# Splitting the first sequence of a fused SSD and MLP kernel into two-token and four-token row groups, with a new instruction order

## The chip, the cores and the metric

The kernel runs on one core of one Trainium2 chip. The metric is the device time of one execution in microseconds. The program has five instruction streams: TensorE (PE, with its weight loads shown as PEld), VectorE (DVE), ScalarE (ACT), GpSimd (POOL) and SyncE (SP), of which SP issues nearly all DMAs.

## The reference

A scan over a sequence with decay (a state-space model in chunked form) feeds a two-layer MLP. There are 4 sequences (`batch`) of 768 tokens and 8 heads; a head has 32 channels of x and 16 states for B and C.

```python
log_a = np.log(np.clip(a, 1e-06, 1.0))
for c in range(nc):                       # chunks of 32 tokens
    cum = np.cumsum(la, axis=-1)
    L = np.exp(cum[:, :, :, None] - cum[:, :, None, :]) * causal
    M = np.einsum('bhin,bhjn->bhij', Cc, Bc) * L
    y_intra = np.einsum('bhij,bhjd->bhid', M, xc)
    y_inter = np.einsum('bhin,bhnd->bhid', Cc, state) * np.exp(cum)[:, :, :, None]
    y[:, :, sl] = y_intra + y_inter
    state = decay_full[:, :, None, None] * state + np.sum(Bx, axis=2)
...
x = y.transpose(0, 2, 1, 3).reshape(3072, 256)
h = x @ w_in                              # 256 x 2048
g = 0.5 * h * (1.0 + np.tanh(c * (h + 0.044715 * h * h * h)))
out = g @ w_out                           # 2048 x 256
```

All inputs and the output are float32 in DRAM.

## The kernel before, in words

The kernel takes chunks of 128 tokens, 24 in all, 6 for each sequence, and works on units `u` of two chunks (12 units, three for each sequence).

**Decay.** Instead of logarithms, the kernel multiplies the clipped `a` from the end of a chunk backwards with one scan (`f_Rq`, `f_R`, line 339). The product R scales B, its reciprocal scales C. `turn` (line 350) transposes 32x32 blocks so that tokens come to lie on partitions. The product over a whole chunk reaches all partitions by a small matmul (`f_ppq`, `f_pp`) and is copied to `pendq` or `pend`; it carries the state from chunk to chunk.

**B and C of the first sequence** are handled in two groups, `GR = ((0, 4), (4, 2))`. Group 0 is chunks 0 to 3 in rows of four tokens: partition p holds tokens 4p to 4p+3, so that a DMA row is 256 bytes. `load_bc0` (149) loads, `f_mulc` and `f_mulb` (417, 424) scale, `f_tw` (429) transposes on TensorE, and `f_ew` (437) copies the result out of PSUM and puts the tokens back in order. Group 1 is chunks 4 and 5 in rows of two tokens (`load_bc1`, `f_mul1`, `f_T1`, `f_ce1`, `f_bh1`, `f_N1`, `f_bn1`, lines 153 and 442 to 475). x of chunks 0 to 3 comes in one load of 512-byte rows in the four-token layout (`load_x4`, 182); a cast makes it bf16 (`f_x4`), `f_XX` (563) puts it in token order by matmuls with a selection matrix `unp`, `f_XD` (575) makes the state products directly from the four-token rows, and `f_xn` copies x out of PSUM.

**The second sequence** scales on POOL or DVE (`f_mul`, 479), transposes on TensorE (`f_T`), copies out (`f_E`), splits C into even and odd heads (`f_F`, 519), transposes B back (`f_N`) and copies (`f_bn`). The third and fourth (`XB`) write the scaled B and C to DRAM (`load_wr`), and read them back transposed (`load_tr`) and plain (`load_bn`).

**One unit** is then: `G` (599), the products of B and C in banks ga and gb; `M` (612), the causal mask on DVE, or for unit 0's second half a copy on ACT (`GE`) and a mask on POOL (`ME`); `D` (629), the state products; `S` and `SP` (677, 689), the running state and its block-diagonal copy; `Y` (642), the output of the scan; `yev` (673), the copy to `xm`. For units 4 to 11, D and G of the next unit are issued together with Y.

**The MLP** of one unit is 8 groups `s1` (708), each of 4 matmuls into one of two PSUM buffers `hp`, each followed by a gelu on ACT (720), and 8 groups `s2` (725), each of 4 matmuls that add into an output bank `o_ps` or `yb`; `oev` copies the output, `store` writes it. The weights come in four quarters each of w_in and w_out (`load_wi`, `load_wo`) and are cast to bf16 in halves (`f_wi`, `f_wo`).

**The order** is written out by hand: `ORDERED` (line 17) names the steps in the order in which they are issued. Each engine takes its own steps in that order. A suffix `:A`, `:D` or `:P` puts a step on ACT, DVE or POOL instead of its usual engine; `~n` is a fill of TensorE with n blocks of 128 columns of zeros, and `+n` puts such a fill ahead of an `s1`. SP's DMAs are issued in the list's order too. There are 192 groups s1 and s2.

Of the kernel before, what the change touches and what calls it, by code (L numbers as in the profile page):

```python
# [8 lines left out]
FP32 = mybir.dt.float32  # L9
# [14 lines left out]
load_bc1.0 load_wo.0 wi.3.0:D gelu.0.1 wi.2.1 s1.0.3 load_x.2 SP.2 pe wi.3.1 gelu.0.2 load_bc.1.1  # L24
gelu.0.3 tp6.2 s1.0.4 load_bc.1.0 gelu.0.4 load_x.3 load_wo.1 xn.3 s1.0.5 s1.0.6 Y.1 gelu.0.5 pp
tp2 gelu.0.6 tp6.3 recip1 s1.0.7 S.1.1 yev.1.0.2 mul1.0:P mul1.1:P tp6.1 pend gelu.0.7 s1.1.0
wo.0.1 T1.0 s1.1.1 T1.1 gelu.1.0 bh1 N1 gelu.1.1 s1.1.2 tp6.0 s1.1.3+10 bn1 ce1.1 load_wo.2
castx.2.None SP.3 wo.0.0 ce1.0 gelu.1.2 gelu.1.3 G.2 s1.1.4 recip.1.4 s1.1.5 gelu.1.4 M.2.1
mul.1.1:P s2.0.0.0.o D.2 M.2.0 load_x.4 gelu.1.5 s2.0.1.0.o s1.1.6 T.1.1 gelu.1.6 S.2.0 s1.1.7
SP.4 Y.2 mul.1.0 yev.2.0.2:D gelu.1.7 wo.1.0 wo.1.1 T.1.0 E.1.1:A castx.3.None:A s1.2.0 wo.2.0  # L30
s1.2.1 E.1.0 wo.2.1 load_wo.3 load_bc.2.1 N.1 gelu.2.0 F.1 s1.2.2 bn.1:D G.3 gelu.2.1 gelu.2.2 D.3
s1.2.3 s2.0.0.1.o S.3.0 S.3.1 load_bc.2.0 gelu.2.3 s1.2.4 M.3.1 s2.0.1.1.o s1.2.5 SP.6 gelu.2.4
s1.2.6 M.3.0 gelu.2.5 wo.3.0:D gelu.2.6 s2.0.0.2.o castx.4.None s1.2.7 Y.3 gelu.2.7 wo.3.1:D
s2.0.1.2.o S.4.0 yev.3.0.2 S.4.1 s2.0.0.3.o oev.0 load_x.5 s1.3.0 s1.3.1 mul.2.1 s2.0.1.3.o
load_wr.2.1 load_x.6 gelu.3.0 gelu.3.1 s1.3.2 oev.1:D SP.8 s1.3.3 s2.1.0.0.o gelu.3.2 M.4.0
gelu.3.3 SP.7 s2.1.0.1.o s2.1.0.2.o s2.1.0.3.o oev.2:D s1.3.4 s1.3.5 s2.1.1.0.o gelu.3.4 M.4.1
mul.2.0:P castx.5.None:A s2.1.1.1.o Y.4 S.5.0 s2.1.1.2.o load_wr.2.0 s2.1.1.3.o load_tr.2.1
load_bn.2 oev.3:D gelu.3.5 s1.3.6 s1.3.7 s2.2.0.0.o yev.4.0.2 load_tr.2.0 gelu.3.6 s1.4.0 SP.9
M.5.1 gelu.3.7 s2.2.0.1.o store.0 store.2 gelu.4.0 s1.4.1 castx.6.None:A s1.4.2 SP.10 s2.2.0.2.o
load_x.7 s2.2.0.3.o gelu.4.1 oev.4:D gelu.4.2 s1.4.3 s1.4.4 load_bc.3.1 s2.2.1.0.o s2.2.1.1.o  # L40
s2.2.1.2.o gelu.4.3 gelu.4.4 s2.2.1.3.o s1.4.5 oev.5 s1.4.6 gelu.4.5 M.5.0 s2.3.0.0.o F.2 store.1
Y.5 s2.3.0.1.o s2.3.0.2.o yev.5.0.2 gelu.4.6 s2.3.0.3.o s1.4.7 S.6.0 gelu.4.7 load_bc.3.0 S.6.1
store.3 s1.5.0 oev.6:D SP.12 s2.3.1.0.o gelu.5.0 s1.5.1 s2.3.1.1.o gelu.5.1 castx.7.None:A
mul.3.1:P s2.3.1.2.o s1.5.2 gelu.5.2 M.6.1 s2.3.1.3.o s1.5.3 M.6.0 Y.6 oev.7:D S.7.0 gelu.5.3
load_x.8 s1.5.4 S.7.1 s2.4.0.0.o s2.4.0.1.o s1.5.5 SP.13 gelu.5.4 load_wr.3.1 yev.6.0.2
castx.8.None store.4 load_x.9 gelu.5.5 SP.14 s2.4.0.2.o s2.4.0.3.o oev.8 s1.5.6 s1.5.7 mul.3.0
castx.9.None s2.4.1.0.o gelu.5.6 load_wr.3.0 gelu.5.7 M.7.0 s2.4.1.1.o s1.6.0 M.7.1 load_tr.3.1
# [38 lines left out]
def kernel(  # L86
# [14 lines left out]
    Q = 128  # L101
# [12 lines left out]
    GR = ((0, 4), (4, 2))  # L114
    R4 = GR[0][1]
    XB = (2, 3)
    P4 = Q // R4

# [88 lines left out]
    bmask = const.tile([128, H * D], BF16, name="bmask")
# [776 lines left out]
```

## Time and profile before

| | us |
|---|---|
| three timed runs | 118.32, 118.58, 119.0 |
| their median | 118.58 |
| span of the profiled execution (first to last instruction) | 116.9 |
| TensorE busy | 110.1 (94%) |
| VectorE busy | 69.4 (59%) |
| ScalarE busy | 72.1 (62%) |
| GpSimd busy | 21.4 (18%) |
| first s1 matmul | 12.50 |
| last s2 matmul's end | 113.9 |

The profile gives the span of the one profiled execution and no other time for it; the median of the timed runs is 1.68 us longer than that span. All times inside the profile count from the span's start. Lines L12 are lines of the kernel before; a busy TensorE includes the fills. In rows of the timeline the first number is the start, the second the length; what stands in brackets is the idle time before the row and what ended it.

### The profile page before, as it was taken

The page shows a single profiled execution, that of the slowest core. Times are in us where ns is not written, and L with a number is a line of the kernel's source. Part 1 is how long each engine was busy: PE and PEld are TensorE (multiplying, and loading weights), DVE is VectorE, ACT ScalarE, POOL GpSimd, SP SyncE. Part 2 cuts the span into 40 slices and gives each one's busy share as a digit, 9 for nine tenths or more (in the row PEclk, how much of TensorE's full clock was granted, in tenths as well). Part 3 has the DMA queues.
Part 4 walks back from the last instruction along what each step waited for, and adds up shares of the span by engine and source line. Part 5 has one row for each costly group of instructions (what it writes and reads, how often), then busy time and mean ns, then how long its engine had stood idle before and what let it go on. Part 6 is the DMA issues. An engine that isn't in the chain of part 4 may idle for free.

```text
span 116.9 us, 3379 instructions
## 1 busy us (share of the span) xinstructions
PE 110.1 (94%) x1426; PEld 92.0 (79%) x1426; DVE 69.4 (59%) x140; ACT 72.1 (62%) x139; POOL 21.4 (18%) x38
## 2 busy tenths in 40 slices
PE   6988999998899999999999999999999999999990
PEld 2354676776789979989898999889798998999970
DVE  5898899899785936716695583049493462101020
ACT  2249899968486459565766677828465587447501
POOL 7606816908206000052200000000000000000000
PEclk9999999999999999999999999999999999999999
DMA  0999997999983929998407472044201201101113
GB/s 26 228 332 357 281 252 178 208 288 257 305 143 90 185 47 219 213 253 200 72 25 171 121 163 63 0 140 98 40 6 63 71 0 52 43 0 50 45 47 132
DMA packets 43007, 15.97 MB, mean 137 GB/s; under 512 B 36657, under 2 KB 41457, under 8 KB 42993
## 3 DMA queue, kind: packets, MB, share of 16 engines
q1 hardware_dynamic: 42800, 15.64, 56.0%
q8 instruction: 11, 0.18, 0.6%
q10 hardware_dynamic: 192, 0.13, 0.5%
q14 instruction: 4, 0.02, 0.1%
HBM read 11.04 MB, written 3.93 MB: 128 GB/s over the span
## 4 chain that ended last, share of the span: by engine, by line
PE 75%; DMA 8%; DVE 6%; SPq 6%; issue 2%; POOL 1%; ACT 0%; DVEq 0%; POOLq 0%
PE o_ps L735 33%; PE hp L717 30%; DMA bcf<-in_B_dram 8%; PE yb L735 3%; SPq L190 3%; PE ga L603 3%; PE yb L658 2%; DVE m L613 2%; PE yb L667 2%; DVE ce L523 1%; SPq L150 1%; DVE bh L327 1%; DVE bc L484 1%; SPq L159 1%; SPq L183 1%
## 5 line engine op out<-in xcount | busy, mean ns | idle before, releaser
L721 ACT ACTIVATE gT<-hp 128x512 bf16<-128x512 f32 x96 | 54.3, 596 | 25.0 <-PE hp L717 24.6
L717 PE MATMUL hp<-xm,w_in_sb 128*128 128x256 bf16 x384 | 53.3, 273 | 0.6 <-ACT gT L721 0.4
L735 PE MATMUL o_ps<-w_out_sb,gT 128*128 128x256 bf16 x352 | 47.3, 273 | 0.0
L717 PEld LDWEIGHTS <-w_in_sb 128*128 128x128 bf16 x384 | 41.4, 114 | 3.5 <-issue 1.9
L735 PEld LDWEIGHTS <-gT 128*128 128x128 bf16 x384 | 37.0, 98 | 4.9 <-issue 1.1
L327 DVE COPY o_sb<-o_ps 128x256 f32<-128x256 f32 x13 | 5.5, 425 | 23.8 <-PE o_ps L735 20.4
L613 DVE TENSOR_TENSOR m<-ga,tri 128x1024 bf16<-128x1024 f32 x12 | 14.6, 1218 | 0.1
L613 DVE TENSOR_TENSOR m<-gb,tri 128x1024 bf16<-128x1024 f32 x11 | 13.4, 1219 | 0.7 <-PE gb L603 0.7
L323 ACT ACTIVATE o_sb<-o_ps 128x256 f32<-128x256 f32 x9 | 3.5, 385 | 9.2 <-PE o_ps L735 9.2
L705 PE MATMUL yb<-wz 128*128 128x512 bf16 (+3 forms) x23 | 7.6, 481 | 1.1 <-DVE wz L220 1.1
L691 DVE SCALAR_TENSOR_TENSOR sp_new<-s_new,pend,bmask 128x256 bf16<-128x256 f32 x17 | 7.9, 476 | 0.0
L327 DVE CAST xm<-yb 128x512 bf16<-128x512 f32 x6 | 4.1, 687 | 5.8 <-PE hp L636 4.8
L684 DVE SCALAR_TENSOR_TENSOR s_new<-s_new,pend,hp 128x64 f32<-128x64 f32 x13 | 3.6, 279 | 6.4 <-PE hp L636 6.2
L705 PEld LDWEIGHTS <-wz 128*128 128x128 bf16 x26 | 3.0, 120 | 5.1 <-issue 3.2
L667 PE MATMUL yb<-m,x 128*32 128x128 bf16 x192 | 6.1, 220 | 0.0
L603 PE MATMUL ga<-ce,bh 32*128 32x256 bf16 x48 | 4.7, 273 | 1.3 <-DVE bn L327 0.9
L484 POOL TENSOR_TENSOR bc<-bc_t,pt 128x768 bf16<-128x768 f32 x2 | 3.0, 1494 | 13.8 <-DMA bc_t<-in_C_dram 13.7
L658 PE MATMUL yb<-ce,sp_new 128*32 128x128 bf16 x160 | 5.3, 221 | 0.0
L603 PE MATMUL gb<-ce,bh 32*128 32x256 bf16 x48 | 4.7, 273 | 0.0
L735 PE MATMUL yb<-w_out_sb,gT 128*128 128x256 bf16 x32 | 4.6, 273 | 0.0
L667 PEld LDWEIGHTS <-x 128*32 128x32 bf16 x192 | 3.8, 97 | 0.8 <-issue 0.8
L323 ACT ACTIVATE xm<-yb 128x512 bf16<-128x512 f32 x6 | 3.6, 595 | 1.1 <-PE hp L636 1.1
(115 smaller groups left out, 79.5 us busy)
## 6 DMA issues: line engine op xcount, KB each, us to landing
out_dram<-o_sb SPq DMA_DIRECT2D x24, 128.0 KB, 1.9
x_t<-in_x_dram SPq DMA_DIRECT2D x20, 128.0 KB, 3.9
wf<-in_moe_w_in_dram SPq DMA_DIRECT2D x4, 512.0 KB, 6.7
wf<-in_moe_w_out_dram SPq DMA_DIRECT2D x4, 512.0 KB, 5.5
bc_t<-in_C_dram SPq DMA_DIRECT2D x3, 384.0 KB, 5.8
bc_t<-in_B_dram SPq DMA_DIRECT2D x3, 384.0 KB, 5.5
scr<-bc SPq DMA_DIRECT2D x4, 192.0 KB, 2.2
x_t<-in_x_dram SPq DMA_DIRECT2D x1, 512.0 KB, 5.8
```

Of the source, the lines that this page charges most:

```text
L323: nc.scalar.activation(o, i, AF.Copy)
L327: nc.vector.tensor_copy(out=o, in_=i)
L484: (nc.gpsimd if eng == "POOL" else nc.vector).tensor_tensor(out=d["bc16"][:, i], in0=d["bc"].rearrange("p i h (r n) -> p i r h n", r=R6)[: ...
L603: nc.tensor.matmul(out=gbank(g)[:, 256 * k:256 * k + 256], lhsT=bh_of(2 * u + k)[gs], rhs=ce_of(2 * u + k)[gs], start=True, stop=True, til ...
L613: nc.vector.tensor_tensor(out=m_of(u)[:, 2 * i:2 * i + 2].rearrange("p g k e t -> p (g k e) t"), in0=gx[i].rearrange("p g (k t) -> p (g k) ...
L658: nc.tensor.matmul(out=y4[32 * j:32 * j + 32, k, w], lhsT=sp[:, 32 * h:32 * h + 32], rhs=ce_of(gc)[:, h % 2], start=first(j), stop=False, ...
L667: nc.tensor.matmul(out=y4[32 * j:32 * j + 32, k, w], lhsT=X16[u][:, k, 32 * h:32 * h + 32], rhs=m[:, h // 2, h % 2, :], start=first(j), st ...
L691: nc.vector.scalar_tensor_tensor(out=sp_new.rearrange("p (g d) -> p g d", g=4), in0=(XN[0][:, H * D:H * D + 64] if gc == 0 else state[("s" ...
L705: nc.tensor.matmul(out=t[:, 0:m * 128], lhsT=wz, rhs=w3.to_broadcast([128, m, 128]), start=True, stop=True, skip_group_check=True)
L717: nc.tensor.matmul(out=hp[:, j * T:(j + 1) * T], lhsT=w_in_k[:, w, q, k], rhs=xm[:, w, u * T:(u + 1) * T], start=(w == 0), stop=(w == 1))
L721: nc.scalar.activation(gts[u][:, 2 * i:2 * i + 2], hps.pop((u, i)).rearrange("p (j t) -> p j t", j=2), AF.Gelu_apprx_tanh)
L735: nc.tensor.matmul(out=ops[gc], lhsT=gts[u][:, fi, k * Q:(k + 1) * Q], rhs=w_out_sb[:, fi, :], start=(fi == 0 and (u > 0 or k == 0)), stop ...
```

## The change

The two groups of the first sequence become `GR = ((0, 2), (2, 4))`: chunks 0 and 1 in rows of two tokens (128 bytes), chunks 2 to 5 in rows of four (256 bytes). x is loaded in token order for every chunk, one load of 128-byte rows for each chunk, so `load_x4`, `f_x4`, `unp`, `c_unp`, `f_XX`, `f_XD` and `f_xn` go; units 0 and 1 use `f_castx` and `f_D` like all others, and chunks 0 and 1 get a transposed-back B (`f_N0`, `f_bn0`). The decays of both groups come from one load each of `aq`, with two clips and two scans; the first sequence no longer needs the long scan. For the other sequences `a` is loaded in four overlapping quarters of 192 to 256 tokens on SP, later than before; one scan over 128 partitions and one `turn` serve all (before: 64 partitions, four turns for `rt` and four for the first sequence). The steps of group 1 are halves (`f_mul1`, `f_ce1`, `f_bh1`, `f_N1`, `f_bn1`). Unit 1 also masks its second half by GE and ME; Y and yev of unit 0 are two halves each. `SP` may run on POOL as two instructions. s2 of unit 1 takes its quarters in turns for its two chunks, as unit 0's did, into bank yb. `ORDERED` is another list.

```diff
-load_aq.0 load_aq.1 load_aq.2 load_aq.3 c_wz load_bc0.1 c_ident c_m4 c_sel c_tri c_zero load_bc0.0
-c_unp load_a.0:A clipq load_x4 Rq tpq recip0 c_cz mulc.0 ~59 tw.1 load_wi.0 c_warm load_a.1:A
-ew.1.1:A mulc.1 c_bmask c_m8 tw.2 mulb ~4 tw.0 peq ew.0.2:A clip ew.0.1 load_wi.1 ew.0.0:A ew.1.2
-c_par ~2 G.0 x4.1 ew.1.0 M.0.0 ~1 ppq GE.2 pendq x4.0:P XX.0 ME.2 XD.0 GE.3 xn.1 ME.3 xn.0:D
-load_wi.2 SP.0 ~17 Y.0 wi.0.1:A wi.0.0:A S.0.0 yev.0.0.2 wi.1.1 XX.1 wi.1.0:A R XD.1 S.0.1
-load_wi.3 S.1.0 s1.0.0 SP.1 xn.2 load_bc1.1 wi.2.0 gelu.0.0 G.1 s1.0.1 s1.0.2 M.1.1 M.1.0
...
+c_wz load_aq.0 c_ident load_aq.1 c_zero c_az c_sel load_aq.3 load_aq.2 c_bmask clipq.0 c_warm
+clipq.1 Rq.0 c_m16 tpq.0 c_cz Rq.1 recipq.0 c_selp load_bc0.1 load_bc0.0 c_m4 peq.0 mulc.1
+load_x.0.0 load_bc1.1 c_tri mulc.0:P ~40 load_x.0.1 mulb tpq.1 tw.2 castx.0.0:D peq.1 recipq.1 ew.2
+tw.0 load_bc1.0 tw.1 ew.1:A ppq.0 ew.0:A ~10 N0 G.0 load_wi.0 load_wi.1 bn0:D mul1.1.0:P mul1.1.1:P
+M.0.0 pendq.0 GE.0.3 castx.0.1:D ~19 T1.1 ~2 D.0 GE.0.2 load_x.1.0 ME.0.3 mul1.0.1 mul1.0.0:P c_par
+SP.0 ~13 T1.0 ce1.0.1:D ce1.0.0:D ME.0.2 load_x.1.1 bh1.1 load_wi.2 S.0.0 Yw.0.0 Yw.0.1 ppq.1 bh1.0
+S.0.1 wi.0.1:D G.1 pendq.1:D yev.0.1.2 yev.0.0.1 M.1.0 wi.0.0 s1.0.0+7 GE.1.2 s1.0.1 load_wi.3
+GE.1.3 ~3 N1.0 wi.1.0:D ce1.1.0:D bn1.0:D gelu.0.0 gelu.0.1 load_wo.0 castx.1.0:A wi.1.1 s1.0.2
+gelu.0.2 load_x.2.0 N1.1 SP.1:P castx.1.1 ~4 D.1 ce1.1.1 S.1.0 s1.0.3+2 gelu.0.3 bn1.1:D G.2 SP.2
+S.1.1 wi.2.1:D load_x.2.1 ME.1.3 ME.1.2 M.2.1 wi.3.1:D wi.2.0 wi.3.0 wo.0.0:D M.2.0 Y.1 s1.0.4+2
+s1.0.5 yev.1.0.2 load_wo.1 wo.0.1 gelu.0.4 gelu.0.5 s1.0.6+7 gelu.0.6 s1.0.7 s2.0.0.0.o load_a.3
+load_a.1 load_wo.2 s1.1.0 s2.0.1.0.o castx.2.None:D gelu.0.7 D.2 gelu.1.0 s1.1.1 load_a.2 load_a.0
+gelu.1.1 S.2.0 SP.4 s1.1.2 load_bc.1.0 wo.1.1:D SP.3:P Y.2 yev.2.0.2:D wo.1.0 s1.1.3 c_ends
+load_bc.1.1 s2.0.0.1.o load_wo.3 gelu.1.2 s1.1.4 gelu.1.3 s2.0.1.1.o wo.2.0:D gelu.1.4 s2.1.0.0.o
+wo.2.1:A s2.1.1.0.o s1.1.5 s2.0.0.2.o clip load_x.3.0 s2.1.0.1.o s1.1.6 s2.0.1.2.o gelu.1.5 R
+load_x.4.0 pe load_x.3.1 s1.1.7 tp6 s2.1.1.1.o gelu.1.6 s2.1.0.2.o mul.1.0 load_x.4.1 gelu.1.7
+wo.3.0 T.1.0 s1.2.0 recip.1 gelu.2.0 s1.2.1 mul.1.1 gelu.2.1 T.1.1 E.1.0 s2.1.1.2.o pp N.1 E.1.1
+wo.3.1:A load_bc.2.1 bn.1:D F.1 s1.2.2 pend castx.3.None:D s2.1.0.3.o s1.2.3 gelu.2.2 s2.0.0.3.o
+s2.0.1.3.o gelu.2.3 oev.2:D castx.4.None G.3 D.3 S.3.0 S.3.1 oev.0 oev.1 s1.2.4 s2.1.1.3.o gelu.2.4
...
-    GR = ((0, 4), (4, 2))
-    R4 = GR[0][1]
+    GR = ((0, 2), (2, 4))
+    R2, R4 = GR[0][1], GR[1][1]
...
     def load_bc0(i):
-        nc.sync.dma_start(out=BC0[0][:, i], in_=(B, C)[i][0, :, 0:R4 * Q, :]
-                          .rearrange("h (p r) n -> p h (r n)", r=R4))
+        nc.sync.dma_start(out=BC0[0][:, i], in_=(B, C)[i][0, :, 0:R2 * Q, :]
+                          .rearrange("h (p r) n -> p h (r n)", r=R2))
...
-    def load_x4():
-        nc.sync.dma_start(out=x4_t, in_=x[0, :, 0:R4 * Q, :].rearrange("h (p r) d -> p h (r d)", r=R4))
...
+        nc.sync.dma_start(out=XF[u][:, k], in_=x[b, :, (c + k) * Q:(c + k + 1) * Q, :]
+                          .rearrange("h p d -> p h d"))
...
+    def c_selp(eng):
+        copy(eng, selp, sel8.rearrange("p (h o) -> p h o", o=1).to_broadcast([128, H, N]))
...
+    def f_N0():
+        t = pso.tile([128, 512], FP32, name="o_ps")
+        T0[("n", 0)] = t.bitcast(BF16)[:, 0:R2 * 128]
+        for c in range(R2):
+            nc.tensor.transpose(out=T0[("n", 0)][:, c * 128:(c + 1) * 128],
+                                in_=bh0[0][:, c * Q:(c + 1) * Q], identity=ident)
...
-    def f_mul1(i, eng):
-        n = GR[1][1]
+    def f_mul1(i, k, eng):
+        rs = slice(2 * k, 2 * k + 2)
...
+    def f_N1(w):
+        T0[("n", 1)] = gx[0][:, w].bitcast(BF16)[:, 0:256]
...
-    def f_SP(gc):
+    def f_SP(gc, eng):
...
+        if eng == "POOL":
+            sc = st.tile([128, 64], FP32, name="sp_s")
+            nc.gpsimd.tensor_scalar(out=sc, in0=s_in, scalar1=pend_of(gc + 1), scalar2=None, op0=ALU.mult)
+            nc.gpsimd.tensor_tensor(out=o, in0=sc.rearrange("p (o d) -> p o d", o=1).to_broadcast([128, 4, 64]),
+                                    in1=m, op=ALU.mult)
...
     def f_s2(u, k, q, pool):
...
-            if u == 0:
+            if u < 2:
                 if k == 0:
-                    ops["0"] = pso.tile([128, 512], FP32, name="o_ps")
+                    ops["u"] = yb if u else pso.tile([128, 512], FP32, name="o_ps")
```

In the new list the third sequence's transposed load of C stands thus ahead of Y.5:

```diff
+gelu.4.2 s2.3.1.1.o M.5.0 s2.3.1.2.o s2.3.1.3.o gelu.4.3 s1.4.4 s1.4.5 gelu.4.4 load_tr.2.1 oev.7:D
+s2.4.0.0.o s2.4.0.1.o castx.6.None s1.4.6 gelu.4.5 F.2 Y.5 S.6.0 gelu.4.6 yev.5.0.2 S.6.1 s1.4.7
```

More of the change, by code (lines that the diff above doesn't have):

```diff
@@ L24 @@
[L24 to L47, printed above, removed]
@@ L263, in c_cz @@
         nc.gpsimd.memset(cz, 0.0)
-    def c_unp():
-        with nc.allow_low_precision("sums of one 1 and zeros"):
-            nc.vector.tensor_reduce(out=sub, in_=ident.rearrange("p (c q) -> p q c", q=P4), op=ALU.add,
-                                    axis=mybir.AxisListType.X)
-        for r in range(R4):
-            nc.vector.tensor_copy(out=unp[:, r, :, r], in_=sub)
     def c_par():
@@ L663, in f_Y @@
             m = MT[u][:, :, k]
-            for w in range(2):
+            for w in ws:
                 for j in range(4):
@@ L836, in sequence @@
     def sequence(b, after):
[L837 removed]
+        mul = {i: add("D", f_mul, b, i, alt="DP", deps=[bl[(b, i)], after] + [rc[b] if i else tp6]) for i in (1, 0)}
         bl[(b, 1)].takes("ld", mul[0], mul[1])
@@ L942 @@
         y.deps = [d for d in y.deps if d is not y]
+    for s in steps.values():
+        if "A" in s.alt and s is not cwarm and s not in aq:
+            s.behind = [*s.behind, cwarm]
+    cwarm.behind = aq
     pools = {"hp": 2, "o": 1, "ga": 1, "gb": 1, "yb": 1, "wf": WFB, "xl": XL, "ld": 2, "ob": 6, "st": 4, "sp": 4}
```

497 lines of the change are left out of this document (251 added, 246 removed).

## The prediction

> **What bounds the kernel now.** I read the busy table by stage first, then the chain that ended last, then the timeline of the first 31 us. The columns of the stage table are the stretch, its length, the busy time of PE, PEld, DVE, ACT and POOL with instruction counts, the granted clock, the DMA share and GB/s.
>
> ```profile
> 12.50:26.10 13.60, 12.91 (x173) 9.69 (x173) 12.45 (x25) 11.62 (x26) 6.77 (x10) 1.00 1.02 230
> 26.10:30.20 4.10, 2.93 (x41) 2.22 (x41) 3.54 (x6) 2.96 (x6) 3.07 (x5) 1.00 1.09 280
> 30.20:113.90 83.70, 83.67 (x1072) 75.00 (x1064) 43.43 (x76) 50.61 (x94) 4.73 (x4) 1.00 0.44 98
> 113.90:116.90 3.00, 0.00 (x0) 0.00 (x0) 0.00 (x0) 0.38 (x1) 0.00 (x0) 1.00 0.39 132
> ```
>
> From 30.2 to 113.9 TensorE has no gap: no order can shorten that stage, only start it earlier or leave it less work. The last 3.0 us are one eviction and its store, and stay. What can be won lies before 30.2. The chain of waits (start, length, what) shows the gap of 26.1 to 30.2:
>
> ```profile
> 24.82 0.48 DVE sp_new L691
> 25.31 0.87 DVE bc L484
> 26.17 0.66 DVE xm L327
> 26.84 0.90 DVE bh L327
> 27.74 1.44 DVE ce L523 x2
> 29.17 0.48 DVE bn L327
> ...
> 35.70 0.87 PE hp L717 x8
> ```
>
> VectorE makes the second sequence's B and C in one serial chain and G.3 waits. Eight matmuls, two groups s1 or s2, take 0.87, so a group costs 0.437. There are 192 groups in all.
>
> **What the dense stage holds.** In the list, 171 groups follow 30.2: 171 x 0.437 = 74.7. The other 9.0 of the 83.7 are nine Y and eight pairs of D and G. At 26.1, after Y.2, 174 groups were left: 76.0 + 9.0 + 0.5 (G.3, D.3) + 0.7 (T.1.0, N.1) = 86.2, so a dense end at 112.3. It came at 113.9: 1.6 were lost there.
>
> **The change by parts.** I follow the new list engine by engine with row durations. Marks in the timeline of before (start, length, engine, line, operation):
>
> ```profile
> 5.40 0.35 DVE L357 RECIPROCAL pt<-rt 128x32 f32<-128x32 f32 x1
> 8.57 1.22 DVE L613 TENSOR_TENSOR m<-ga,tri 128x1024 bf16<-128x1024 f32 x1
> 10.72 0.47 DVE L691 SCALAR_TENSOR_TENSOR sp_new<-o_ps,pendq,bmask 128x256 bf16<-128x256 f32 x1
> 12.50 0.60 PE L717 MATMUL hp<-xm,w_in_sb 128*128 128x256 bf16 x4
> ```
>
> *To M.0.0.* Today clipq starts at 4.25 because c_unp holds VectorE; aq has landed at about 3.25 (ACT issue near 1.25 plus 2.0). c_unp goes and selp (1.19 on DVE) moves to ACT, so clipq.0 starts near 3.4. There are now two clips (0.21), two scans (0.42) and smaller turns, and c_m4 and peq.0 (0.19 + 0.28) stand before mulc.1: recipq.0 ends at 5.35 against 5.75, mulc.1 starts at 5.9 against 5.84. With two rows a token group the mulb is 256 wide, not 512 (0.42 for 0.68), and mulc.0 runs on POOL. All three ew (0.38 each) are serial on ACT and end at 7.85; N0, bn0 (0.42) and G.0 follow; M.0.0 starts at 8.7 against 8.57. No gain here.
>
> *To the first s1.* XX and XD leave (8 and 32 matmuls for each u, 0.8 from 9.35 to 10.13), but M.0.0 is followed on VectorE by castx.0.1 (256 wide; half of the 0.42 row for 512), mul1.0.1 (0.42), c_par (0.2) and SP.0 (0.47): SP.0 ends at 11.0 to 11.4, against 11.19. POOL has mul1.1 twice (0.62 each, after recipq.1 at 8.05), ME.0.3, mul1.0.0, ME.0.2 (0.63, 0.62, 0.63) and ends at 11.2. Y.0 ends at 12.0. ACT then does bh1.1, bh1.0 and two yev, 0.38 each: 13.2. So s1.0.0 starts at 13.2, **0.7 later** than 12.50.
>
> *To Y.2.* ACT is now the pace: GE.1.2 and GE.1.3 (0.59 each) stand before gelu.0.0, so that ends at 15.0; castx.1.0 and ce1.1.1 (0.38, 0.48) come between later gelu (0.60). The bank that N1.0 writes is free only when M.1.0 ends (14.0 to 14.7), bn1.0 ends at 15.1 to 16.0, D.1 runs at 16.0, SP.2 ends near 17.3, Y.1 near 18.0 (17.2 today), s1.0.7 at 20.85, Y.2 at **23.6** (26.1 today). By then 13 groups are done, against 18.
>
> *The rest.* 179 groups x 0.437 = 78.2, plus 9.0, 0.5, three transposes (T.1.0, T.1.1, N.1; 0.34 each) and pp 0.2: 88.9. Dense end 23.6 + 88.9 = 112.5, against 113.9. The front itself wins nothing (112.5 against 112.3); the gain is that the second sequence's chain is covered. VectorE has clip 0.25, R 0.68 (between 0.42 for 128 and 0.94 for 384), pe 0.33, tp6 0.57, mul 0.95, recip 0.43, mul 0.95, two E 0.96, bn 0.54, F up to 1.52: 8.1 from about 25.2, so 33.3, and 34.5 with T.1 and N.1 in PE's order. Between Y.2 and G.3 PE now has 22 groups, most of them s2 of u 0 and 1: G.3 is due at 34.6. If that cover is gone, the 1.6 is back.
>
> *DMA.* x of the first four chunks goes in 128-byte rows instead of 512-byte ones. What the queues moved in 17.1:18.1 (128-byte rows) and in 6.3:7.5 (512-byte rows), and the row of a late load (KB, us to landing):
>
> ```profile
> DMA packets 1064, 0.14 MB, mean 141 GB/s; under 512 B 1062, under 2 KB 1062, under 8 KB 1064
> DMA packets 685, 0.38 MB, mean 320 GB/s; under 512 B 14, under 2 KB 659, under 8 KB 685
> bcf<-in_B_dram SPq DMA_DIRECT2D x1, 128.0 KB, 8.9
> ```
>
> A load of 1,024 short rows costs about 0.95; the one load of 512-byte rows cost 1.8. So x costs 3.8 for 1.8, and four SP issues of 0.45 for one of 0.75. The loads of a leave the ACT queue and come on SP behind wo.1 and wo.2; only the second sequence needs them. Adding rows in SP's order: bc1.1 lands at 7.7, x.0.1 8.6, bc1.0 9.6 to 10.1 (wanted at 10.05), wi.0 11.0, wi.2 15.6 (16.2), wo.1 22.3 (23.3), a 25.1 (25.2), bc.1.0 26.6 (27). Little slack, no stall. The Trainium skill (DMA: Bandwidth & Descriptors, Specifications) wants 512 B or more for line rate, which speaks against this change; the two rows agree.
>
> *Later.* Twelve SP (0.48) go from VectorE to POOL, as two instructions I put at 0.9 (the 0.62 row for 256, plus a 64-wide one between 0.1 and 0.3). VectorE is busy 43 of 83.7 there, so it is worth nothing. The third sequence's transposed load is now issued three groups before Y.5; its landing is 2.8 to 4.7 in the rows for ch, which gives a stall of 0 to 0.6. Evictions that stand behind a gelu cost another 0 to 0.3. I take 0.4 for both and for the DMA's slack, so the end is at 112.9 and the span is 115.9, 1.0 less. The page gives the span alone; the median of the runs is 1.68 above it, and I keep that: **117.6**.
>
> **Rivals.**
>
> *Better.* VectorE rows overlap by about 0.07 (M pairs start 1.14 apart and last 1.22). If the front holds that and the 0.4 is not lost, the span is 114.6: 116.3. Chance 0.13.
>
> *POOL against VectorE.* Rows:
>
> ```profile
> 27.65 1.52 DVE L523 TENSOR_SCALAR ce<-ch,par 128x768 bf16<-128x768 bf16 x2
> 48.73 0.74 DVE L523 TENSOR_SCALAR ce<-ch,par 128x768 bf16<-128x768 bf16 x2
> ```
>
> The same pair took 1.52 with a POOL cast beside it (27.67 to 28.96) and 0.74 without. In the new front mul1.0.1 on VectorE meets mul1.0.0 and ME.0.2 on POOL; held until 11.2 it is 1.1 late, SP.0 and G.1 with it, s1.0.0 near 13.8. Of that 0.5 to 0.9 reaches the end: 118.3. Chance 0.17. The Trainium skill (SBUF — State Buffer, SBUF: two separate sides) calls the pair's port an exclusive lock; the rows agree.
>
> *Half clock.* The fill steps by 0.43 until 5.7:
>
> ```profile
> 5.30 0.15 PEld L705 LDWEIGHTS <-wz 128*128 128x128 bf16 x1 [0.28 <-issue]
> 5.73 0.56 PEld L705 LDWEIGHTS <-wz 128*128 128x128 bf16 x3 [0.28 <-issue]
> ```
>
> The new first fill has 40 blocks, not 59, and ends near 5.3, before that point; then PE is nearly idle to 7.9. If the step stays slow until 9 or later, 29 blocks, G.0 and the transposes cost about 2 more, of which 0.6 reaches SP.0: 118.2. Chance 0.07. The Trainium skill (TensorE: Matmul & The Clock Gate, Part 1) says one busy window of about 3.4 us releases the clock, at a phase that varies; 4.2 us of fill would do by that rule.
>
> *Slower: bc1.0 late.* It is the sixth load; mul1.0.1 waits for it, and VectorE's SP.0, so Y.0, stand behind it with no cover. Each us past 10.1 is a us at the end. The first 1.0 eats the gain; from a landing at 11.7 on the change is slower by 0.5%. For: bcf loads issued behind others landed after 7.5 and 8.9, and one SP issue took 2.81. Against: those stood behind 2 MB of weights, these before them. Issued at 5.5 with 7.5 it lands at 13.0, 2.9 late: 120.5. Chance 0.18.
>
> **Numbers.** Forecast 117.6 with 0.45, its own range 116.8 to 118.3. A difference below 0.5% (118.0 to 119.2) is about what a measurement can't tell from none. Faster: 0.13 + 0.39 = 0.52. Same: 0.05 + 0.17 + 0.06 = 0.28. Slower: 0.18 and a 0.02 rest. The range 116.2 to 119.5 leaves out most of the slower case and the best of the better one.
>
> **What would show it.** First s1 matmul at 13.2 (14 or more: port or bc1.0; see what ended SP.0's wait). Y.2 at 23.6 with 13 groups behind it. No wait of G.3 on VectorE; PE dense from 24 to 112.9. Wrong, if PE shows gaps between 24 and 60, or if x and wi land over 1 us later than listed.

## The result and the profile after

The changed kernel takes 122.53 us (median of 4 runs, 121.56 to 123.26), the kernel before 118.79 on the same chip. The ratio is 1.033, with a 95% interval of 1.025 to 1.040. So it is slower by 3.7 us, where 1.0 faster was forecast. The executions of the changed kernel lie further apart than those of the old one; ratios are therefore given with their intervals, and a profile is one execution. Ratios leave out executions that took over 1.5% more than the fastest of the same kernel.

The profiled execution of the changed kernel took 122.64, with a span of 120.0 (116.9 before). Its busy table and the shares of its chain by engine and by line, from the page:

```profile
PE 111.0 (93%) x1371; PEld 92.4 (77%) x1371; DVE 64.6 (54%) x130; ACT 70.5 (59%) x137; POOL 34.8 (29%) x71
...
PE 57%; DMA 16%; SPq 15%; DVE 3%; issue 2%; ACT 2%; POOL 1%; POOLq 0%
PE hp L705 25%; PE o_ps L723 21%; DMA ch<-scr 7%; PE yb L723 6%; DMA wf<-in_moe_w_in_dram 5%; SPq L192 5%; SPq L184 4%; DMA scr<-bc 4%; PE ga L578 2%; PE yb L638 2%; SPq L515 2%; PE yb L647 1%; SPq L733 1%; ACT gT L709 1%; SPq L158 1%
```

TensorE is busy for 0.9 more than before and the span is 3.1 longer, so most of the loss is waiting. The same line of the page of before:

```profile
PE 75%; DMA 8%; DVE 6%; SPq 6%; issue 2%; POOL 1%; ACT 0%; DVEq 0%; POOLq 0%
```

The shares of DMA and SP in the chain have doubled: `ch<-scr` is the transposed load of C (the third and fourth sequences), `scr<-bc` the write that it reads, and `wf` are the weights. VectorE, which stood in the old chain with B and C of the second sequence, went from 6% to 3%.

What TensorE waited for (total, times, longest):

```profile
PE o_ps L723 <- DVE o_sb L332: 1.2, 1, 1.2
PE ga L578 <- DVE ce L533: 1.2, 1, 1.2
...
PE hp L705 <- POOL w_in_sb L330: 0.2, 1, 0.2
```

And the two large waits on VectorE's side and on TensorE's, from the timeline (start, length, engine, line, operation; in brackets the idle time before and what ended it):

```profile
56.23 0.75 DVE L533 TENSOR_SCALAR ce<-ch,par 128x768 bf16<-128x768 bf16 x2 [2.78 <-DMA ch<-scr]
57.03 0.28 PE L578 MATMUL ga<-ce,bh 32*128 32x256 bf16 x2 [1.24 <-DVE ce L533]
79.78 0.75 DVE L533 TENSOR_SCALAR ce<-ch,par 128x768 bf16<-128x768 bf16 x2 [4.00 <-DMA ch<-scr]
80.44 0.42 DVE L332 COPY o_sb<-o_ps 128x256 f32<-128x256 f32 x1
80.91 0.60 PE L723 MATMUL o_ps<-w_out_sb,gT 128*128 128x256 bf16 x4 [1.24 <-DVE o_sb L332]
```

Read them in pairs. At 56.2 F.2 (L533) starts when the third sequence's C has landed, and the G in Y.5 follows 1.24 late. At 79.8 F.3 starts when the fourth sequence's has landed. TensorE does not need F.3 there: it needs the eviction `oev.13` (the L332 row), which stands behind F.3 in VectorE's queue and holds the output bank. Together 2.48.

Marks of the front and the end, as forecast and as measured in this execution (a quarter is there when the cast that waits for it starts):

| | forecast | measured |
|---|---|---|
| M.0.0 starts | 8.7 | 8.55 |
| first s1 | 13.2 | 13.15 |
| first quarter of w_in is there | 11.0 | 11.75 |
| third quarter of w_in is there | 15.6 | 17.4 |
| Y.2 starts | 23.6 | 24.39 |
| last matmul ends | 112.9 | 116.7 |

G.3 starts at 35.90 and waits for nothing, as forecast. The lateness shows in the weights' casts:

```profile
13.48 0.61 POOL L330 CAST w_in_sb<-wf 128x512 bf16<-128x512 f32 x1 [1.12 <-DMA wf<-in_moe_w_in_dram]
17.42 0.61 POOL L330 CAST w_in_sb<-wf 128x512 bf16<-128x512 f32 x1 [0.34 <-DMA wf<-in_moe_w_in_dram]
19.43 0.87 POOL L330 CAST w_in_sb<-wf 128x512 bf16<-128x512 f32 x1 [1.40 <-DMA wf<-in_moe_w_in_dram]
20.86 0.87 POOL L330 CAST w_out_sb<-wf 128x512 bf16<-128x512 f32 x1 [0.56 <-DMA wf<-in_moe_w_out_dram]
```

Each of these casts waits for its weights: the last three quarters of w_in and the first of w_out. The chain that ended last runs through them too (start, length, what):

```profile
9.31 3.87 SPq L192
13.23 6.15 DMA wf<-in_moe_w_in_dram
19.43 0.87 POOL w_in_sb L330
20.30 0.54 issue
20.86 0.88 POOL w_out_sb L330
```

SP comes to the end of its issue of the fourth quarter only at 13.2, and the quarter lands 6.15 later. In the kernel before SP had issued all four by 7.2.

### The profile page after: what moved, and what is told of

Same layout as the page of the kernel before. It is cut to its first block, busy times and chain, and to the rows that moved or that the text cites. A ratio compares the mean times of both kernels' runs of the same rounds, so it can differ in the third digit from the quotient of the medians.

```text
span 120.0 us, 3320 instructions
## 1 busy us (share of the span) xinstructions
PE 111.0 (93%) x1371; PEld 92.4 (77%) x1371; DVE 64.6 (54%) x130; ACT 70.5 (59%) x137; POOL 34.8 (29%) x71
## 4 chain that ended last, share of the span: by engine, by line
PE 57%; DMA 16%; SPq 15%; DVE 3%; issue 2%; ACT 2%; POOL 1%; POOLq 0%
PE hp L705 25%; PE o_ps L723 21%; DMA ch<-scr 7%; PE yb L723 6%; DMA wf<-in_moe_w_in_dram 5%; SPq L192 5%; SPq L184 4%; DMA scr<-bc 4%; PE ga L578 2%; PE yb L638 2%; SPq L515 2%; PE yb L647 1%; SPq L733 1%; ACT gT L709 1%; SPq L158 1%
## 5 line engine op out<-in xcount | busy, mean ns | idle before, releaser
L723 PE MATMUL o_ps<-w_out_sb,gT 128*128 128x256 bf16 x320 | 43.6, 273 | 1.3 <-DVE o_sb L332 1.2
L332 DVE COPY o_sb<-o_ps 128x256 f32<-128x256 f32 x10 | 4.2, 423 | 24.7 <-PE o_ps L723 21.5
L678 POOL TENSOR_SCALAR sp_s<-s_new,pend 128x64 f32<-128x64 f32 x10 | 4.7, 470 | 29.1 <-DVE s_new L667 16.3
L588 DVE TENSOR_TENSOR m<-gb,tri 128x1024 bf16<-128x1024 f32 x10 | 12.2, 1215 | 0.0
L693 PE MATMUL yb<-wz 128*128 128x512 bf16 (+3 forms) x25 | 8.2, 462 | 1.0 <-DVE warm L222 1.0
L723 PE MATMUL yb<-w_out_sb,gT 128*128 128x256 bf16 x64 | 8.8, 273 | 0.0
L330 POOL CAST x<-x_t 128x512 bf16<-128x512 f32 (+1 forms) x7 | 4.3, 619 | 14.1 <-DMA x_t<-in_x_dram 14.1
L679 POOL TENSOR_TENSOR sp_new<-sp_s,bmask 128x256 bf16<-128x256 f32 x12 | 8.1, 672 | 1.0
L328 ACT ACTIVATE xm<-yb 128x512 bf16<-128x512 f32 (+1 forms) x10 | 5.4, 557 | 2.8 <-PE hp L615 2.4
L533 DVE TENSOR_SCALAR ce<-ch,par 128x768 bf16<-128x768 bf16 x6 | 2.2, 416 | 6.8 <-DMA ch<-scr 6.8
```

The source lines that it names most:

```text
L328: nc.scalar.activation(o, i, AF.Copy)
L588: nc.vector.tensor_tensor(out=m_of(u)[:, 2 * i:2 * i + 2].rearrange("p g k e t -> p (g k e) t"), in0=gx[i].rearrange("p g (k t) -> p (g k) ...
L679: nc.gpsimd.tensor_tensor(out=o, in0=sc.rearrange("p (o d) -> p o d", o=1).to_broadcast([128, 4, 64]), in1=m, op=ALU.mult)
L693: nc.tensor.matmul(out=t[:, 0:m * 128], lhsT=wz, rhs=w3.to_broadcast([128, m, 128]), start=True, stop=True, skip_group_check=True)
L723: nc.tensor.matmul(out=ops[gc], lhsT=gts[u][:, fi, k * Q:(k + 1) * Q], rhs=w_out_sb[:, fi, :], start=(fi == 0 and (u > 1 or k == 0)), stop ...
```

## The experiments

The theory (T in the expectations): the transposed loads of C are issued too late, which costs 2.5, and the small rows of x make the weights late, which eats what the new front won. The rivals: POOL slows VectorE all along (R1), the front is the whole loss (R2), the weights are late by their place in the list and not by the rows (R3). All ratios are against the kernel before on the same chip; 1% is 1.18 us.

| kernel | ratio | 95% interval |
|---|---|---|
| the change | 1.033 | 1.025 to 1.040 |
| e1 early round trips | 1.011 | 1.007 to 1.015 |
| e2 F.3 behind oev.13 | 1.017 | 1.011 to 1.023 |
| e3 state products on VectorE | 1.034 | 1.030 to 1.038 |
| e4 wide rows of x | 1.020 | 1.015 to 1.025 |
| e5 before, late round trip | 1.022 | 1.016 to 1.028 |
| e6 before, gap filled | 1.002 | 0.999 to 1.005 |
| e7 e1 with weights ahead of x | 1.039 | 1.034 to 1.045 |
| e8 e1 and e4 together | 1.002 | 1.000 to 1.005 |
| e9 e1, cast behind SP.9 | 1.016 | 1.010 to 1.022 |
| e10 e9, longer fill | 1.014 | 1.010 to 1.018 |

### e1: the round trips issued earlier

```diff
-M.3.0 M.3.1 s1.2.5 ... SP.6:P s2.2.0.1.o ... load_x.5.1 M.4.0
+M.3.0 M.3.1 recip.2 s1.2.5 ... SP.6:P mul.2.1:P s2.2.0.1.o ... load_x.5.1 load_wr.2.1 M.4.0
-load_wr.2.0 load_x.8.0 ... gelu.4.4 load_tr.2.1 oev.7:D
+load_wr.2.0 load_tr.2.1 load_x.8.0 ... gelu.4.4 oev.7:D
-load_bn.3 store.8 store.11 store.7 ... store.10 load_tr.3.1
+load_bn.3 load_tr.3.1 store.8 store.11 store.7 ... store.10
```

> The changed kernel with the round trip of the late C columns issued earlier: the reciprocal and the product of the third sequence right behind M.3.1, its DRAM write behind x.5.1, its transposed load behind the other write (some 7 us earlier than 52.1), and the transposed load of the fourth sequence before four stores (some 3 us earlier than 75.3). The arithmetic is the same; the product of the third sequence runs on POOL instead of VectorE. Theory T (the two 1.24-us waits of TensorE at 57 and 81 us are the loss, because nothing else is late behind them): both waits go, the end comes 2.5 earlier, 122.5 to 120.0 us; still slower than before, 118.8, by what the tail and the front lost. Rival R1 (products on POOL slow VectorE all along, and the waits are only where it shows): the waits come back at another place, gain under 0.8, 121.8 or more. Rival R2 (the front is what costs): no gain over 0.5.

Measured 1.011: 2.2% of 118.3, or 2.6 us, of the loss is gone (by e9 and e10, which hold the same edit, 2.0 to 2.2). Both waits are gone. T holds in mechanism and size; R1 and R2 as the whole fall. (The edit also moves the third sequence's product from VectorE to POOL; e5 moves the load alone.) In its place came a small wait (0.23 in this profile, 0.46 in e8's) for SP.9 on POOL, which e9 takes up. The profiled execution was the longest of the seven (121.92): a weight quarter came so late that TensorE waited 1.86 before 22.0.

### e2: F.3 behind the eviction

```diff
-... s2.6.1.2.o F.3 gelu.7.3 s2.6.1.3.o gelu.7.4 oev.13:D load_x.11.1
+... s2.6.1.2.o gelu.7.3 s2.6.1.3.o gelu.7.4 oev.13:D F.3 load_x.11.1
```

> The changed kernel with one entry moved: F.3, the VectorE product that waits for the fourth sequence's transposed load, stands behind the eviction oev.13 in VectorE's queue instead of ahead of it. No transfer moves. Theory T (the second wait of TensorE is only that eviction queued behind the waiting product): the wait at 80.9 goes, 1.2 us less, 121.3; the wait at 57 stays. Rival (the transposed load itself is late for TensorE too): the wait moves some 1.3 us down to chunk 9's first G and is 0.5 or more there; gain under 0.7.

The wait at 81 is gone and nothing took its place; the one at 57 is still there. TensorE's waits in this kernel:

```profile
PE hp L436 <- DVE cz L420: 1.2, 1, 1.2
PE ga L578 <- DVE ce L533: 1.1, 1, 1.1
...
PE hp L693 <- ACT gT L709: 0.2, 1, 0.2
```

So the fourth sequence's load was late for VectorE's queue only, not for TensorE's own need. The size is less sure. The ratio gives a gain of 1.6% or 1.9 us, more than the 1.24 of the wait; the median of all six executions (121.19, from 119.41 to 126.39) gives 1.026, a gain of 0.6. The profiled execution is the shortest of the six, and its last matmul ends 2.2 earlier than the change's: 1.24 is the wait, 0.11 a shorter first wait, 0.7 is Y.2 at 23.70 for 24.39, though nothing in front was touched, and 0.2 is not traced. The 0.7 is the spread of the front between executions.

### e3: the state products back on VectorE

```diff
-SP.1:P SP.3:P SP.6:P SP.8:P SP.9:P SP.12:P ... SP.22:P
+SP.1 SP.3 SP.6 SP.8 SP.9 SP.12 ... SP.22
```

> The changed kernel with all twelve state products that it runs on POOL put back on VectorE at the same places of the list. Theory T: the two waits at 57 and 81 stay; VectorE's casts and products beside POOL's (0.88 against 0.42, 0.78 against 0.48) become short again, but each state product costs VectorE about 0.48: between 0.5 faster and 0.5 slower, 122.0 to 123.0. Rival R1 (VectorE slowed by POOL is the loss): 1.5 or more faster, 121.0 or less.

Measured 1.034, the same as the change. The profile shows two parts that cancel. From Y.2 to the last matmul's end it took 90.75 (26.17 to 116.92) for the change's 92.30, and 1.49 of the 1.55 are shorter waits: the one at 57 is 0.99, and the one at 81 is gone, against T. TensorE came 1.8 later here, the fourth sequence's load went out as early as before (74.98 for 75.31), and F.3 no longer held the eviction up. Nothing else behind Y.2 changed (0.06), so there R1 falls. The front lost the 1.8: TensorE waited 1.8 for weights, in three waits, and 0.74 ahead of Y.2 for a state product on VectorE. What the products on POOL do to the front is not separated from the weights here.

### e4 and e8: wide rows of x

```diff
 def load_x(u, k):
...
+    if u < 2:
+        if k == 0:
+            nc.sync.dma_start(out=XF[u].rearrange("p c h d -> p (c h d)").rearrange("p (h e) -> p h e", e=2 * D),
+                              in_=x[b, :, c * Q:(c + 2) * Q, :].rearrange("h (p r) d -> p h (r d)", r=2))
+        return
```

> The changed kernel, but x of the first four chunks is loaded in 256-byte rows, two tokens a row, with one load for two chunks, as the kernel before does; the rest is unchanged, so the tokens of these chunks' x stand in another order than their B and C (this part of the computation is changed). It shows what the 128-byte rows of x in front cost. Theory T (the weight quarters are late because the DMA engines are filled with small rows and SP waits to issue): the third and fourth quarters of the first weight land 1 to 2 us earlier than in the changed kernel (17.4 and 19.4), Y.2 is 0.5 to 1.2 earlier than 24.4, and the end as much: 121.3 to 122.0; the two waits at 57 and 81 stay. Rival R3 (weights are late by their place in the list or by the casts of x on VectorE, not by the rows): quarters land within 0.5 of the changed kernel's, no gain, 122.2 to 122.8.

> The early round trips and the wide rows together: the changed kernel with the transposed loads issued earlier, and x of the first four chunks loaded in 256-byte rows, two tokens a row (so these chunks' x stands in another token order than their B and C, which changes that part of the computation). Theory T (two separate faults, the late round trips and the small rows in front, make the whole miss): the gains add, 2.6 and some 1.0 to 1.5, to 117.5 to 118.3, about the forecast. Rival (one hides the other): no faster than with the early round trips alone, 119.0 to 119.6.

Measured 1.020 and 1.002, so the wide rows are worth 1.3% on the change and 0.8% on e1: 1.0 to 1.5 us, as T says. (The kernel before has 512-byte rows there, not 256, so e4 goes half of the way back. It also has two loads of x where the change has four; width and number of the loads were not varied apart.) What the queues moved from 3.3 to 16 us, in the change, in e4, and in the kernel before:

```profile
DMA packets 8810, 2.82 MB, mean 222 GB/s; under 512 B 8062, under 2 KB 8062, under 8 KB 8809
```

```profile
DMA packets 7009, 3.53 MB, mean 278 GB/s; under 512 B 5962, under 2 KB 5962, under 8 KB 7009
```

```profile
DMA packets 6254, 3.80 MB, mean 300 GB/s; under 512 B 4059, under 2 KB 5147, under 8 KB 6253
```

The change sends 41% more packets than before and 26% fewer bytes in the same time; the time of its packets is 104% of what 16 engines have there, for 103% before and 108% in e4, so the engines are full in all three. e4 gets 0.71 MB more through in those 12.7 us, more than a weight quarter. SP has issued all four quarters by 8.6, and POOL casts the third and fourth one behind the other, at 17.4 and 18.0, with no wait for them:

```profile
17.43 1.36 POOL L335 CAST w_in_sb<-wf 128x512 bf16<-128x512 f32 x2
```

R3 falls. Yet Y.2 came no earlier in e4's profile (24.53): in that execution TensorE's matmuls were slow from 8 to 10.9 (see the last section), and the first s1 came at 14.09 for 13.15. The 0.7 by which its span is shorter lies behind Y.2, where the two waits are 0.71 and 1.11. So e4 alone does not show the gain in Y.2. e8 does: its Y.2 came at 24.11, with the same slow matmuls and the first s1 at 14.17, and those of e10, e9 and e1, which have the small rows, at 25.02, 25.22 and 27.00.

The chains say the same. In the profiles of the change, e1, e2, e9 and e10 the chain that ended last runs through the fourth quarter of w_in; in e4 and e8 it holds no weight load. And Y.2 follows the cast of the fourth quarter: that started at 18.68, 19.43, 20.08 and 20.17 in e2, the change, e10 and e9, and Y.2 came 4.9 to 5.1 later in each. In e1 the cast was at 21.07, and Y.2, with slow matmuls, 5.9 later.

e8 takes both faults away and comes out level with the kernel before, short of the 117.5 to 118.3 that was expected. 3.9 us of loss (3.3%) are then 2.6 for the trips, 1.0 for the rows and 0.3 that stays, of which SP.9's wait of 0.46 in its profile may be all.

### e5: the late trip put into the kernel before

```diff
-s2.1.1.3.o load_tr.2.1 load_bn.2 ... s2.3.0.0.o F.2 store.1 Y.5
+s2.1.1.3.o load_bn.2 ... s2.3.0.0.o store.1 load_tr.2.1 F.2 Y.5
```

> The kernel before, with two entries moved: the transposed load of the third sequence's C, which it issues at 38.5, is issued behind store 1 at about 48, and F.2, which waits for it, follows at once. Nothing else is changed. Theory T (the round trip issued late is what costs): at the changed kernel's 4.1 us from issue to landing it lands at 52.1, F.2 takes 0.75, and Y.5's G, at 51.7 before, waits until about 53.0: 1.2 slower, the loss of the changed kernel made in the old one. Rival (the old order hides it, as it does half-landed transfers elsewhere): under 0.4 slower.

Measured 1.022, 2.6 us, for an expected 1.2. The mechanism is the expected one, F.2 first and then G:

```profile
47.66 1.22 SPq L504 DMA_TRANSPOSE ch<-scr  x1
```

```profile
53.37 0.75 DVE L522 TENSOR_SCALAR ce<-ch,par 128x768 bf16<-128x768 bf16 x2 [5.24 <-DMA ch<-scr]
```

```profile
54.17 0.28 PE L602 MATMUL ga<-ce,bh 32*128 32x256 bf16 x2 [3.09 <-DVE ce L522]
```

The load was issued where expected, but took 5.7 from issue to landing and not 4.1. The old list issued it at 38.5 for a use at 48.7, so even such a landing would have been covered.

### e6: the old gap at G.3

```diff
-F.1 s1.2.2 bn.1:D G.3 gelu.2.1 gelu.2.2 D.3 s1.2.3 s2.0.0.1.o ... M.3.1 s2.0.1.1.o s1.2.5
+F.1 s1.2.2 bn.1:D s2.0.0.1.o s2.0.1.1.o G.3 gelu.2.1 gelu.2.2 D.3 s1.2.3 ... M.3.1 s1.2.5
```

> The kernel before, with two groups of the second multiplication (s2 of chunk 0, steps 0.1 and 1.1, 0.43 each) moved ahead of G.3, which leaves TensorE idle for 0.89 at 28.8 to 29.7. Every step of G.3's chain on VectorE stays where it is. Theory T (the 0.89 is a gap in the old kernel that work at hand can fill, so the changed kernel's new front was not needed for it): 0.85 faster, 117.2 where before takes 118.07. Rival: the groups push G.3 or the states behind it back, and the time is as before within 0.3.

Measured 1.002: nothing won, against an expected 0.85, and within the 0.3 of the rival. One reason is in e5, whose list is that of the kernel before up to 38 us. The rows of G.3 there:

```profile
28.15 0.60 PE L716 MATMUL hp<-xm,w_in_sb 128*128 128x256 bf16 x4
28.90 0.28 PE L602 MATMUL ga<-ce,bh 32*128 32x256 bf16 x2
```

and VectorE's F.1 ahead of it:

```profile
27.60 0.74 DVE L522 TENSOR_SCALAR ce<-ch,par 128x768 bf16<-128x768 bf16 x2
```

G.3 at 28.90 and no wait over 0.2, where the profile of before had G.3 at 29.69 after a wait of 0.89. The difference is F.1: 0.74 here, 1.52 there. In the profile of before a POOL cast started 0.02 behind F.1 (27.67); here it starts 0.39 behind (27.99). e6's own profile has a third value: POOL casts run from 26.74 to 29.76, and F.1 beside them took 1.10. So the gap differs between executions, and the 0.89 is the largest of the three recorded. The later runs of the kernel before agree: 34 of 45 have spans of 115.8 to 116.6, not 116.9. The other reason is in e6's profile. G.3, behind the two groups, waited for nothing, but from Y.2 to the last matmul's end it took 88.1 (26.68 to 114.82), for 88.4 in the profile of before (25.46 to 113.87): filling the gap won 0.3 there. (That execution was the longest of its twelve, 119.79; its Y.2 came 1.2 later, where the list is the old one.) The Trainium skill (SBUF — State Buffer, SBUF: two separate sides) calls the port that VectorE and POOL share an exclusive lock; a pair that takes twice as long or not at all longer, by 0.4 us in the start of its neighbour, agrees with that. No run here moved the cast alone, so the cause of the 1.52 is argued, not shown.

### e7: the weights ahead of x

```diff
-load_wi.1 ... load_x.1.0 ... load_x.1.1 bh1.1 load_wi.2 ... s1.0.1 load_wi.3
+load_wi.1 load_wi.2 load_wi.3 ... load_x.1.0 ... load_x.1.1 bh1.1 ... s1.0.1
```

> The kernel with the early round trips (119.3 by its ratio), with the third and fourth quarter of the first weight issued ahead of x of chunks 2 and 3. Theory T (the DMA engines are full, so what is put first only pushes the other back): the quarters land 1 to 2 us earlier, x of chunk 2, cast at 14.8 now, lands 2 to 4 us later, TensorE waits for it ahead of Y.1, and the time is 1 to 3 us longer, 120.3 to 122.3. Rival R3 (the quarters are late by their place in the list alone): faster by 0.5 or more, 118.8 or less.

Measured 1.039, 3.4 us slower than e1, a little beyond what T expected. x of chunk 2 lands at 20.1 and TensorE waits for it:

```profile
20.52 0.25 PE L615 MATMUL hp<-x,bn 128*32 128x64 bf16 x4 [3.38 <-ACT x L328]
```

Part of the 3.4 is TensorE's clock: all four executions have a mean granted clock of 0.967 to 0.986 (see the last section). The earlier landing that T expected does not show in the casts, for POOL and VectorE came to the third and fourth quarter only at 22.2 and 22.7. Of the two orders the list's own is the better; what is put first delays the other, as T says.

### e9 and e10: a cast behind SP.9, and a longer fill

```diff
-load_x.7.1 castx.7.None SP.9:P gelu.4.1
+load_x.7.1 SP.9:P castx.7.None gelu.4.1
```

```diff
-... c_tri mulc.0:P ~40 load_x.0.1
+... c_tri mulc.0:P ~48 load_x.0.1
```

> The kernel with the early round trips, and the cast of x of chunk pair 7 put behind SP.9 in POOL's queue. In the two kernels with the early trips this cast waits for x (to 55.84 and 53.35), because the earlier transposed load holds SP for 2.6 to 2.8 us ahead of that x, and SP.9 behind it makes TensorE wait 0.23 and 0.46. Theory T (the early trip moved a small wait to POOL's queue): that wait goes, 0.2 to 0.5 faster than with the early trips alone (1.0107 of before), 1.006 to 1.009. Rival: x is needed as early as before and the wait shows at the next chunk, ratio 1.010 or more.

> The same, with the first fill of TensorE eight columns groups longer (48 for 40, two more matmuls of 512 columns). In the profile of the wide-rows kernel the matmuls behind the fill took 0.39 to 0.42 until about 10.9 us, and 0.28 from 6.3 on in the other profiles of this front, though the fill was the same 4.45: the half-clock rival in one execution. If such executions are a part of the spread (118.8 to 121.9 with the early trips), the longer fill makes the runs closer together and the median 0.2 to 0.5 lower than without it; if not, it is the same within 0.3.

e9's wait is gone: TensorE has no wait of 0.2 or more after 24.1. Its waits in full, from 0.2 up:

```profile
PE yb L693 <- DVE warm L222: 1.0, 1, 1.0
PE hp L436 <- DVE cz L420: 0.8, 1, 0.8
PE hp L705 <- POOL w_in_sb L330: 0.6, 1, 0.6
PE hp L705 <- ACT ge L597: 0.6, 1, 0.6
PE hp L693 <- ACT gT L709: 0.2, 1, 0.2
PE hp L615 <- ACT gT L709: 0.2, 1, 0.2
PE hp L615 <- POOL x L330: 0.2, 1, 0.2
```

But the time is no shorter (1.016 against 1.011, intervals that overlap): Y.2 came at 25.22, and the front's spread is larger than the 0.2 to 0.5 looked for. e10 gives 1.014, the same, so the longer fill does nothing that can be measured; neither of the two profiles had slow matmuls to cure. Both are misses as improvements. As traces they are the clean ones: from Y.2 to the last matmul's end e9 takes 114.75 - 25.22 = 89.53 and e10 114.56 - 25.02 = 89.54.

No version ran faster than the kernel before; e8, which changes part of the computation, is level with it.

## Why the prediction was wrong, by its own steps

Two of its own signs of being wrong came: a gap of TensorE between 24 and 60 (the wait at 57), and a weight quarter over 1 us later than listed.

**To the first s1: right in the number.** 8.55 for 8.7 and 13.15 for 13.2. The last step is in part luck: ScalarE's yev ended at 12.74, not 13.2, and TensorE then had G.1 and a fill still to run, from 12.31 to about 13.15. B for chunks 2 to 5 (bc1.0), the rival "Slower", came in time: mul1.0.1 ran at 10.12.

**POOL against VectorE: seen, and cheap.** mul1.0.1 took 0.83 for 0.42 beside POOL, as that rival said, and SP.0 still ended at 11.5. e3 shows that the products on POOL cost nothing behind Y.2.

**DMA, "Little slack, no stall", and with it "To Y.2: ACT is now the pace": failed.** The forecast added rows at fixed prices and had the third quarter of w_in at 15.6; it came at 17.4, and the fourth, which it did not list, at 19.4. From 3.3 to 16 the queues moved 222 GB/s, and SP, which the sum gave 0.45 for an issue of x, was held in its issues:

```profile
4.20 1.61 SPq L184 DMA_DIRECT2D x_t<-in_x_dram  x1
9.31 4.39 SPq L192 DMA_DIRECT2D wf<-in_moe_w_in_dram  x2
16.66 3.87 SPq L196 DMA_DIRECT2D wf<-in_moe_w_out_dram  x1
```

Two weight issues took 4.39 and one 3.87, where one at 21.50 took 0.42, and every load behind them in the list went out later by that. That full engines are what holds SP is a reading of these rows, and no run tests it alone. What set Y.2 was then not ScalarE but the fourth quarter. Y.2 was 0.8 late in this execution, 0.1 to 1.6 in the profiles of e2, e9 and e10 with the same front, and 3.4 in e1's. e4 and e8 price the rows at 1.0 to 1.5. The forecast cited the rows against the change, had 2.0 more of DMA time for x in its own sum (3.8 for 1.8), ahead of the weights, and let them cost nothing.

**The rest after Y.2: right.** 88.9 and the 0.4 of "Later" make 89.3; e9 and e10, without the waits, took 89.5. G.3 did not wait. The changed kernel took 116.7 - 24.4 = 92.3: 2.5 of that are the two waits, 0.3 stays unexplained.

**"Later", 0 to 0.6 for the third sequence: the step that failed most.** Its landing was in the range given: 4.1, for 2.8 to 4.7. The forecast does not show how it came from these landings to 0 to 0.6; what the measured rows need beside the landing is F.2 itself. Issue at 52.14, landing at 56.2, F.2 0.75, G at 57.03; TensorE was ready for it at 57.03 - 1.24 = 55.79, 3.65 after the issue. The issue was counted as "three groups before Y.5" in the list, while SP got to it in its own time. The chain has the steps:

```profile
44.01 4.28 DMA scr<-bc
48.35 0.64 SPq L520
49.05 0.54 SPq L184
49.63 1.78 SPq L515
51.47 0.57 SPq L177
52.14 4.06 DMA ch<-scr
```

B's write to DRAM landed at 48.3 (`scr<-bc`), as SP came to the plain load that reads it. SP then issued that load, a load of x, another transposed load (1.78) and a load of C, and only then this one. With those rows the stall is landing plus F.2 less 3.65: 4.1 + 0.75 - 3.65 = 1.2, and 1.8 at the upper end of the same range. The fourth sequence was not looked at at all; there the load goes out at 75.31, behind four stores and an x. Its price came by a way that no price list shows, an eviction queued behind a product that TensorE did not need yet.

**"1.6 were lost there": in part chance.** Of the 0.89 that TensorE waited for G.3, most came from F.1's 1.52, in the one execution that was profiled; in the two other profiles of that front F.1 took 0.74 and 1.10. The forecast read those two rows for F.1 (1.52 and 0.74) as a rival's price, and did not ask whether the gap it wanted to win back was made of the same thing. e5 has the old front without it, and e6 wins nothing by filling it. So the change had less to win than 1.0 from the start: e5's dense end less its wait is 116.33 - 3.09 = 113.24, 0.6 before the 113.9 that the forecast counted from, which leaves some 0.4 (an estimate from these ends).

Adding up for the last matmul in the profiled execution: 0.8 for Y.2, 2.5 for the two waits, 0.6 for the rest less the 0.4 that was allowed is 3.5; 0.3 is unexplained; 116.7 - 112.9 = 3.8. To the time it is 0.3 more for the tail (3.3 for 3.0) and 1.0 for the time around the span (2.64 for 1.68; in the other three runs 1.8 to 1.9).

## What to carry to other kernels

When a list is written anew, follow each round trip through DRAM on its own: time of issue in the issuing queue, landing at its slowest, the work on the landed data, and then what TensorE is doing. And look behind the instruction that waits: an eviction queued there can stop TensorE, though the waiting data are not due yet. Before a gap is counted as a gain, ask whether the durations that make it are the usual ones; two rows of the same instruction at 1.52 and 0.74 are a warning.

## What the runs showed of the hardware

**TensorE's clock fell again in mid-run.** The granted clock in e1's profile (stretch, length, busy times of PE, PEld, DVE, ACT and POOL, then the clock):

```profile
20.00:22.00 2.00, 0.14 (x1) 0.00 (x1) 0.43 (x1) 0.04 (x1) 0.87 (x1) 1.00 0.86 197
22.00:24.00 2.00, 2.00 (x13) 1.62 (x14) 1.66 (x3) 1.19 (x2) 1.55 (x3) 0.66 0.74 249
24.00:26.00 2.00, 2.00 (x13) 1.16 (x12) 0.70 (x1) 0.60 (x1) 1.31 (x4) 0.50 0.80 226
26.00:28.00 2.00, 2.00 (x48) 1.70 (x45) 1.35 (x4) 1.09 (x2) 0.40 (x5) 0.98 0.85 229
```

After the wait of 1.86 the clock was at 0.5 for some 3 us, and a group of four matmuls took 0.85 for 0.44. So a late weight cost its wait and then about 0.9 more, by Y.2's distance from the fourth quarter (5.9 for 5.0). e7 did the same after its 3.38 (0.50 from 20 to 26). e8 shows 0.50 from 8 to 10, after a wait of 1.28 behind the first fill, and e4 the same slow matmuls (0.39 to 0.42 for 0.28) after a wait of 0.81, with a clock recorded as full. On the other side e2 and e3 kept 1.00 after 1.18 and 1.19 at that place, the changed kernel after its two waits of 1.24, and e5 after 3.09. So the rival "Half clock", with its chance of 0.07, did happen in two of the nine profiles with this front, and the runs without a profile say that such falls are common: 23 of the 57 executions with this front have a mean granted clock below 0.99, and 1 of the 57 of the kernel before and e6. In the changed kernel itself it is one of four (0.984 at 122.41, no longer than the others), so its loss is not the clock's. In e9 three such executions took 120.42 to 122.5, for 119.30 to 119.73 at 1.00; in e1 three took 118.83 to 119.74 and one 121.92, for 118.85 to 119.78. No run changes the clock alone, so its price is open. The Trainium skill (TensorE: Matmul & The Clock Gate, Part 1) has the clock fall after about 3.4 us without work, at a phase that varies; no fall after 3.09 agrees with that, falls after 1.86 and 1.28 do not, and what decided is open.

**Transposed loads vary.** From issue to landing those of C took 4.1 to 4.4 in the changed kernel, 2.8 to 4.7 in the profile of before, 2.8 in e6's, and 5.7 at the longest, in e5.
